# Float32r products of 128 rows as pairs of 64-row products on the two row halves of TensorE

## The chip, the cores and the metric

The kernel runs on one core of a Trainium2 chip (TensorE, VectorE, ScalarE, GpSimdE, SyncE and the DMA engines of that core). The metric is the device time of one launch in microseconds (us). The profile's names are used for the engines: PE is TensorE's matmuls, PEld its weight loads, DVE is VectorE, ACT is ScalarE, POOL is GpSimd, SP is SyncE, whose queue issues most DMAs.

## The reference

Windowed causal attention over 8 batches and 8 heads (576 positions, head dimension 64), and then a gated feed-forward network over all 4608 tokens. All data is float32.

```python
scores = np.where(mask, scale * q @ k.T + bias, -1e9)      # rel >= 0 and rel < 128
attn = softmax(scores) ; x = attn @ v                       # x: 4608 x 512
gate = 1.0 / (1.0 + np.exp(-(x @ w_gate)))                  # 512 x 1536
val = x @ w_val                                             # 512 x 1536
out = gate * val @ w_out                                    # 1536 x 512
```

## The kernel before

The program has four stages on PE: attention (scores, transposes, values), the first feed-forward blocks (line L913), the remaining feed-forward blocks (L1103), and last the product with `w_out` (L1290). Only the last stage changes.

The last stage multiplies a 3 x 3 grid of blocks by a scheme that needs fewer block products than the plain one: 15 products, named 0 to 14, over sums and differences of blocks of the hidden layer. It runs three times (`last(t)` for t = 0, 1, 2, called a third below), each for 1536 tokens. In a third the 15 products follow each other in the order of the text of `last`. They add into PSUM accumulators, the chains "A" to "F", with two banks each (j = 0 and 1, the two halves of 128 output columns). After a product, `then(j)` takes what is wanted out of its bank: a copy on ACT (`snap`, L1215; `fork`, L1220) or a multiply-add on DVE (`plus`, L1233).

A product has a contraction of 512, cut in four chunks of 128 rows. Float32 is kept by splitting each operand in a high and a low float32r part and multiplying three of the four pairs. So one product and one j is a group of 12 matmuls, each of 128 rows, 128 stationary columns and 512 moving columns into one PSUM bank; such a matmul with its weight load is called a record here. There are 15 x 3 x 2 = 90 groups. The moving operand is `duo`, a ring of four buffers (`RING`), two for each product (q = 0 and 1, two chunks each). The high part is a cast (`copy`, L326 on ACT or L327 on DVE) or a negated copy (L1256), the low part a subtraction on DVE (`minus`, L335, or L1257). Before some products `sums` (L1191) forms differences of blocks, on DVE, each on two halves. Products 13, 3 and 7 have one such pair of operations, products 4, 1 and 14 two. The stationary operand is `wo`, prepared earlier. `load` fetches blocks by DMA.

The order of all instructions is made by a planner, `Graph.order`: `g.add` gives each operation its engine, an assumed cost, what it reads and writes, and a priority (`want`). PE work in the order of the text has one priority (1.0e6); the planner takes what is ready first. Each engine then runs its instructions strictly in the planned order, with semaphores between engines.

At the very end (t = 2, product 14) the group j = 1 is done in two pieces of 256 columns (`last_six`, L1277). The key "seam" makes the first group of the last stage come behind matmuls of L1103 that read it.

Of the kernel before, what the change touches and what calls it, by code (L numbers as in the profile page):

```python
# [8 lines left out]
F32 = mybir.dt.float32  # L9
# [6 lines left out]
P = 128  # L16
B, H, S, D = 8, 8, 576, 64
# [7 lines left out]
NB = 512  # L25
# [10 lines left out]
NB9 = NT // NB  # L36
# [14 lines left out]
POOL = (0, 1, 6, 7)  # L51
# [16 lines left out]
EAGER, WARM = 30.0, 45.0  # L68
NEAR = 4.0
END = 2 * P  # L70
COLD, SLOW = 10.3, 0.85
FIRST_LAND = 0.9
LATE = 4.0
# [92 lines left out]
class Graph:  # L166
# [122 lines left out]
    def emit(self, o):  # L289
        o.made = o.emit()  # L290
        if o.after:
            self.tc.add_manual_dep(o.made.ins, o.after.made.ins.name, mybir.DependencyInfo(mybir.DependencyClass.Sync, mybir.DependencyReason.DATA), reason="port")
# [11 lines left out]
def attention_gated_ffn(ctx: ExitStack, tc: tile.TileContext, qd, kd, vd, wg, wv, wo, out):  # L304
    nc = tc.nc
# [61 lines left out]
    nc.gpsimd.iota(rel[:, 0], [[-1, P]], base=0, channel_multiplier=1, allow_small_or_imprecise_dtypes=True)  # L367
    ident = const.tile([P, P], F32, name="ident")
    make_identity(nc, ident)
    little = const.tile([P, TRI], F32, name="little")  # L370
    nc.gpsimd.memset(little, 1.0e-9)
    spare = {}
# [797 lines left out]
    def kept_at(slot):  # L1170
# [3 lines left out]
        n = 4 if tag[0] == "h" else 1  # L1174
        return T(moe, f"part_{tag}", [P, n, NB], F32, tag=tag)[:, i]

    def last(t):
        F = FIRST + 2
        rows, left = {}, {}

        def load(name, of=None):
            slots = [stage_free.pop(0) for _ in range(2)]
            rows[name] = slots
            for q, slot in enumerate(slots):
                move(lambda slot=slot: staged(slot), lambda q=q: hid[of or name, t, q],
                     [hid_key(of or name, t, 2 * q + m, i) for m in range(2) for i in range(4)], [("row", *slot)], F, 512, True)
# [7 lines left out]
        def drop(*names):  # L1194
            for name in names:
                stage_free.extend(rows.pop(name))
# [14 lines left out]
        def snap(name, chain, j):  # L1211
            keep_at((name, j))
            b = bks[chain, j]
            o = val((name, j))
            g.add("ACT", act_cost(NB, psum=True), lambda: nc.scalar.mul(o(), mm[b], 0.5), [("mm", b)], [key((name, j))], F)  # L1215
# [6 lines left out]
        def plus(o, chain, a, j, scale=0.5, op=ADD, fresh=False, cols=slice(NB)):  # L1222
            b, va = bks[chain, j], val((a, j))
            if fresh:
                keep_at((o, j))
                writes, reads = [key((o, j))], [key((a, j))]
                vo = val((o, j))
            else:
                writes, reads, vo = [key((a, j))], [], va
                held_at[o, j] = held_at.pop((a, j))  # L1230
            n = cols.stop - (cols.start or 0)
            b, at = (apart[0], slice(n)) if apart and cols.start else (b, cols)
            g.add("DVE", dve_cost(n, psum=True), lambda: nc.vector.scalar_tensor_tensor(  # L1233
                vo()[:, cols], mm[b][:, at], scale, va()[:, cols], op0=ALU.mult, op1=op), [("mm", b), *reads], ["tail"] if apart and cols.start else writes, F)
# [4 lines left out]
        def store(name, m, n, j, cols=slice(NB)):  # L1239
            r, c = (2 * m + j) * P, (3 * t + LABEL[3 * t:3 * t + 3].index(n)) * NB  # L1240
            v = val((name, j))
            x, y = cols.start or 0, cols.stop
            move(lambda: out[r:r + P, c + x:c + y], lambda: v()[:, cols], ["tail" if x else key((name, j))], [("out", r, c + x)], F, (y - x) / 2)
            if y == NB:
                free(name, j)

        def product(p, chain, name, then, minus_=False):
            ring = []
            for q in range(2):
                slot = rows[name][q]  # L1250
                r = RING[ducks[0] % len(RING)]
                ducks[0] += 1
                duo = lambda part_, r=r: T(moe, f"duo{r}", [P, 2, 2, NB], F32R, tag=f"ar{HOME[r]}")[:, part_]
                hi, lo, v = (lambda duo=duo: duo(0)), (lambda duo=duo: duo(1)), (lambda slot=slot: staged(slot))
                if minus_:
                    g.add("ACT", act_cost(2 * NB), lambda hi=hi, v=v: nc.scalar.mul(hi(), v(), -1.0), [("row", *slot)], [("ar", r, 0)], F)  # L1256
                    g.add("DVE", dve_cost(2 * NB, two=True), lambda hi=hi, lo=lo, v=v: nc.vector.scalar_tensor_tensor(  # L1257
                        lo(), v(), -1.0, as32(hi()), op0=ALU.mult, op1=SUB), [("row", *slot), ("ar", r, 0)], [("ar", r, 1)], F, port=True)
                else:
                    copy(hi, v, 2 * NB, [("row", *slot)], [("ar", r, 0)], F)  # L1260
                    minus(lo, v, lambda hi=hi: as32(hi()), 2 * NB, [("row", *slot), ("ar", r, 0)], [("ar", r, 1)], F, pool=False)
                ring.append((r, duo))
            for j in range(2):
                start = (chain, j) not in bks
                if start:
                    bks[chain, j] = bank()
                b = bks[chain, j]
                if t == NB9 // 3 - 1 and p == ORDER[-1] and j:
                    plus("a1", chain, "a1", j, cols=slice(END, NB))
                    apart.append(bank())  # L1270
                    for cols, b, at in ((slice(0, END), b, slice(0, END)), (slice(END, NB), apart[0], slice(0, NB - END))):
                        def last_six(cols=cols, b=b, j=j, at=at):
                            for q, (r, duo) in enumerate(ring):
                                for m in range(2):
                                    for e, (xp, wp) in enumerate(((0, 0), (0, 1), (1, 0))):
                                        z, i, part_ = unit(p, 2 * q + m, wp)
                                        nc.tensor.matmul(mm[b][:, at], wo2(z, part_)[:, i, j * P:(j + 1) * P], duo(xp)[:, m, cols],  # L1277
                                                         start=cols.start > 0 and q == m == e == 0, stop=q == 1 and m == 1 and e == 2, skip_group_check=True)
                        g.add("PE", 12 * ((cols.stop - cols.start) / 2400 + 0.0133), last_six,
                              [("ar", r, x) for r, _ in ring for x in range(2)] + sorted({("wo", *unit(p, k, w)[::2]) for k in range(KC) for w in range(2)}), [("mm", b)], 1.0e6)  # L1280
                        then(j, cols)
                    continue
                for q, (r, duo) in enumerate(ring):
                    units = {(m, w): unit(p, 2 * q + m, w) for m in range(2) for w in range(2)}

                    def six(q=q, duo=duo, b=b, j=j, units=units, start=start):
                        for m in range(2):
                            for e, (xp, wp) in enumerate(((0, 0), (0, 1), (1, 0))):
                                z, i, part_ = units[m, wp]
                                nc.tensor.matmul(mm[b], wo2(z, part_)[:, i, j * P:(j + 1) * P], duo(xp)[:, m],  # L1290
                                                 start=start and q == 0 and m == 0 and e == 0, stop=q == 1 and m == 1 and e == 2, skip_group_check=True)
                    g.add("PE", 6 * (NB / 2400 + 0.0133), six, [("ar", r, 0), ("ar", r, 1)] + sorted({("wo", z, part_) for z, _, part_ in units.values()}),
                          [("mm", b), *(["seam"] if t == 0 and p == ORDER[0] else [])], 1.0e6)
                then(j)
# [19 lines left out]
        sums("q2", "q2", "10", SUB)  # L1314
        product(4, "F", "q2", lambda j: plus("y11", "F", "a2", j))
        drop("q2")
        product(9, "E", "12", lambda j: (plus("y11", "E", "y11", j, -0.5), store("y11", 1, 1, j), snap("y12", "E", j)))
        drop("12")
        load("00")
        product(6, "B", "00", lambda j: (plus("y00", "B", "y00", j), store("y00", 0, 0, j)))  # L1320
        if t == 0:
            g.add("PY", 0.0, lambda: None, [("row", *rows["01"][1])], ["first rows"], F)
            for z in range(len(SLOTS), len(SLOTS) + len(LATER)):
                fetch_o(z, ["first rows"])
        load("q10")
        product(10, "C", "q10", lambda j: plus("y12", "C", "y12", j), True)
        load("22")
        sums("00", "22", "00", SUB)
        product(7, "B", "00", lambda j: plus("y02", "B", "y02", j))
        sums("q10", "01", "q10", SUB)  # L1330
        drop("01")
        sums("q10", "q10", "00", SUB)
        product(1, "C", "q10", lambda j: (plus("y02", "C", "y02", j), store("y02", 0, 2, j)))
        drop("q10")
        product(8, "B", "22", lambda j: (plus("y12", "B", "y12", j), store("y12", 1, 2, j)))
        drop("22")
        load("q5")
        sums("q5", "10", "q5", SUB)
        sums("q5", "q5", "00", SUB)
# [173 lines left out]
```

## Time and profile before

| | |
|---|---|
| median of 3 runs | 937.11 us (936.88 to 937.45) |
| profiled execution | 937.64 us, of which the span from first to last instruction is 935.9 us |
| PE | 926.5 us busy (99% of the span) |
| DVE | 783.9 us busy (84%) |
| ACT | 516.2 us busy (55%) |
| POOL | 207.5 us busy (22%) |

The sum of the prediction is made against the profiled execution's own 937.64 us, 0.53 us above the median. A busy share is an average over all stages: PE is without a gap in the last stage, and POOL's 22% lies almost all before it.

### The profile page before, as it was taken

How to read it: one execution, taken by the hardware profiler on the slowest of the kernel's cores; microseconds unless marked ns; L12 is line 12 of the kernel's file. 1: busy time of each engine (PE TensorE's matmuls, PEld its weight loads, DVE VectorE, ACT ScalarE, POOL GpSimd, SP SyncE). 2: the span in 40 equal slices, each digit the busy share in tenths (PEclk: the TensorE clock that was granted, in tenths of full speed). 3: DMA queues.
4: the chain of work that ended last, by engine and by line, in shares of the span. 5: the costliest groups of instructions: out<-in, count | busy, mean ns of one | idle time of the engine just before them, and what ended most of it. 6: DMA issues, size and time to landing. Idle time of an engine off the chain costs nothing.

```text
span 935.9 us, 18859 instructions
## 1 busy us (share of the span) xinstructions
PE 926.5 (99%) x6602; PEld 790.5 (84%) x6602; DVE 783.9 (84%) x1855; ACT 516.2 (55%) x1334; POOL 207.5 (22%) x394
## 2 busy tenths in 40 slices
PE   8999999999999999999999999999999999999998
PEld 7888888888878888888889999988888888888887
DVE  7999888898898998867888696774698998898896
ACT  8998888899874454324454363544454343333432
POOL 5644436554631000103021212212110000000000
PEclk9999999999999999999999999999999999999999
DMA  8787668966756445579798889879798571463531
GB/s 322 243 275 257 219 225 291 302 222 222 238 136 218 166 145 152 119 217 225 220 224 282 241 218 336 201 222 303 199 286 277 155 277 57 158 223 148 157 113 68
DMA packets 91631, 200.27 MB, mean 214 GB/s; under 512 B 10000, under 2 KB 28688, under 8 KB 91152
## 3 DMA queue, kind: packets, MB, share of 16 engines
q1 hardware_dynamic: 79728, 179.86, 56.4%
q0 software_dynamic: 11520, 18.88, 13.5%
q8 instruction: 52, 0.85, 0.4%
q10 hardware_dynamic: 288, 0.33, 0.1%
q14 instruction: 43, 0.35, 0.1%
HBM read 118.03 MB, written 81.00 MB: 213 GB/s over the span
## 4 chain that ended last, share of the span: by engine, by line
PE 92%; DVE 3%; ACT 1%; POOL 1%; issue 1%; DMA 1%; POOLq 0%; DVEq 0%
PE mm L1103 23%; PE later L1103 22%; PE later L1290 15%; PE mm L1290 10%; PE mm L913 9%; PE area L671 4%; PE mm L734 3%; PE mm L785 3%; PE mm L823 1%; POOL pt L796 1%; ACT pb L582 1%; DVE area L688 1%; DVE pb L578 1%; PE mm L783 1%; DVE pb L775 0%
## 5 line engine op out<-in xcount | busy, mean ns | idle before, releaser
L1103 PE MATMUL later<-xc,w2s 128*128 128x512 f32 (+1 forms) x1008 | 225.4, 371 | 0.0
L1103 PE MATMUL mm<-xc,w2s 128*128 128x512 f32 (+1 forms) x1008 | 225.0, 371 | 0.0
L1103 PEld LDWEIGHTS mm<-xc,w2s 128*128 128x128 f32 x1008 | 184.7, 188 | 26.4 <-DVE later_hs L1120 0.2
L1103 PEld LDWEIGHTS later<-xc,w2s 128*128 128x128 f32 x1008 | 184.6, 188 | 26.5
L913 PE MATMUL mm<-first,first 128*128 128x512 f32 x480 | 127.1, 404 | 0.0
L1290 PE MATMUL later<-duo,wo 128*128 128x512 f32 x432 | 100.7, 389 | 0.0
L861 POOL DMA_DIRECT2D hidq<-later_hs x47 | 41.2, 905 | 260.9 <-DVE later_hs L1120 141.0
L913 PEld LDWEIGHTS mm<-first,first 128*128 128x128 f32 x480 | 85.1, 189 | 16.0 <-ACT spread L326 0.6
L1290 PEld LDWEIGHTS later<-duo,wo 128*128 128x128 f32 x432 | 81.1, 188 | 16.8
L582 ACT ACTIVATE pb<-pb,st 128x128 f32<-128x128 f32 x216 | 84.7, 396 | 3.6 <-DVE st L578 3.0
L1290 PE MATMUL mm<-duo,wo 128*128 128x512 f32 x324 | 75.7, 389 | 0.0
L1290 PEld LDWEIGHTS mm<-duo,wo 128*128 128x128 f32 x324 | 60.8, 188 | 12.6
L1115 ACT ACTIVATE sg<-later 128x512 f32<-128x512 f32 (+3 forms) x55 | 27.4, 512 | 57.1 <-PE later L1103 40.9
L796 POOL TENSOR_SCALAR_AFFINE_SELECT pt<-early_h 128x384 f32<-128x384 f32 x96 | 49.3, 536 | 40.4 <-ACT early_h L326 14.4
L796 POOL TENSOR_SCALAR_AFFINE_SELECT pt<-spread 128x384 f32<-128x384 f32 x96 | 49.4, 540 | 38.4 <-ACT spread L326 15.3
L1115 ACT ACTIVATE sg<-mm 128x512 f32<-128x512 f32 (+3 forms) x53 | 27.5, 526 | 49.0 <-PE mm L1103 36.2
L734 PEld LDWEIGHTS mm<-pt,vr 64*64 64x64 f32 x1056 | 41.1, 133 | 10.5 <-POOL st L765 3.2
L1110 DVE TENSOR_TENSOR later<-later,low 128x512 f32<-128x512 f32 (+1 forms) x48 | 31.3, 652 | 21.9 <-PE later L1103 21.5
L326 ACT COPY low<-mm 128x512 f32<-128x512 f32 (+1 forms) x45 | 24.6, 550 | 45.2 <-PE mm L1103 29.3
L1110 DVE TENSOR_TENSOR mm<-mm,low 128x512 f32<-128x512 f32 (+1 forms) x48 | 31.2, 651 | 19.4 <-PE mm L1103 16.8
L734 PE MATMUL mm<-pt,vr 64*64 64x192 f32 (+2 forms) x1056 | 45.2, 284 | 0.8 <-POOL pt L796 0.8
L578 DVE CUSTOM_DVE_ANT_0 pb<-area,early_h 128x128 f32<-128x128 f32 x198 | 45.2, 286 | 0.7
(258 smaller groups left out, 1646.7 us busy)
## 6 DMA issues: line engine op xcount, KB each, us to landing
hid<-later_hs SPq DMA_DIRECT2D x38, 256.0 KB, 3.6
vr<-in_v_dram SPq DMA_DIRECT2D x32, 288.0 KB, 5.0
hidq<-later_hs POOLq DMA_DIRECT2D x36, 256.0 KB, 6.0
wraw<-in_moe_w_gate_dram SPq DMA_DIRECT2D x14, 512.0 KB, 5.1
wraw<-in_moe_w_val_dram SPq DMA_DIRECT2D x14, 512.0 KB, 4.8
wraw<-in_moe_w_out_dram SPq DMA_DIRECT2D x12, 512.0 KB, 6.1
rows_xr<-hidq SPq DMA_DIRECT2D x11, 512.0 KB, 5.0
w2s<-stash SPq DMA_DIRECT2D x6, 896.0 KB, 9.5
```

Source lines behind the costliest of these rows:

```text
L578: g.add("DVE", 0.21, lambda: nc.vector.tensor_tensor_reduce(pb()[:, e], from_(), relm[u.p][:, w], op0=ALU.add, op1=ALU.min, scale=-0.125, ...
L582: g.add("ACT", 0.39, lambda: nc.scalar.activation(pb()[:, e], pb()[:, e], AF.Exp, bias=st()[:, e:e + 1], scale=-1.0, accum_out=st()[:, 3 + ...
L671: nc.tensor.matmul(squares()[h * D:(h + 1) * D, a:a + n], qraw(u)[rows, i - r * MID, h * D:(h + 1) * D], keys, start=True, stop=True)
L734: nc.tensor.matmul(mm[both[h].at][e * D:(e + 1) * D, a - e * S - cuts[h]:b - e * S - cuts[h]], vraw(u)[r * D:r * D + D, c], seen, start=fi ...
L785: nc.tensor.transpose(mm[z.at][:, e * P:(e + 1) * P], pb()[:, e], ident)
L796: return nc.gpsimd.affine_select(pt(u)[:, f0:f0 + 2 * n - 1:2, :], both(), [[0, n], step], cmp, 0.0, base=0, channel_multiplier=mult)
L861: g.add("POOL", 1.2, lambda to=to, of=of: nc.gpsimd.dma_start(to(), of(), accum_op=ALU.add), keys, parts_, F, size=2 * kb / 300.0, port=False)
L913: nc.tensor.matmul(mm[s.at][:, 0:wd], w.tile(kind, wi, i)[:, c * P:(c + 1) * P], xpart(x, c)[:, 0:wd], start=(k == 0 and c == 0), stop=(k ...
L1103: nc.tensor.matmul(mm[b][:, 0:N2], w.tile2(i, wp)[:, wk, c * P:(c + 1) * P], combo(k, xp, N2)[:, c], start=(start and c == 0 and j == 0), ...
L1110: g.add("DVE", dve_cost(N2, psum=True), lambda: nc.vector.tensor_tensor(o(), bk(b)(), a(), op=ALU.add), [("mm", b), *reads] if okeys else ...
L1115: g.add("ACT", act_cost(y - x, psum=True), lambda x=x, y=y, s=s: nc.scalar.activation(sg[h]()[:, x:y], bk(b)()[:, x:y], AF.Tanh, scale=0.5 ...
L1290: nc.tensor.matmul(mm[b], wo2(z, part_)[:, i, j * P:(j + 1) * P], duo(xp)[:, m], start=start and q == 0 and m == 0 and e == 0, stop=q == 1 ...
```

## The change

In the last stage every record but those of the very last product for j = 0 and 1 at t = 2 becomes two matmuls of 64 rows: one on rows 0 to 63 (r = 0), one on rows 64 to 127 (r = 1). 88 groups (1056 records) become 2112 half matmuls. Both halves of a record add into the same bank. The half on rows 64 to 127 is issued 16 records behind (8 steps of two records, `BEHIND`), so that the two halves that stand next to each other in the program mostly write different banks. Where a group's second half begins, it waits for a semaphore of POOL: a memset of one column of a small tile `passed`, which itself waits for the end of the group's first half. `then(j)` is planned after the group's second half. Before the very last product, `run_out` issues the 16 outstanding second halves alone. The order of the 12 records in a group is changed (four records with the high part of `duo` stand first), and the order of the products in a third is changed in its second half.

```diff
+BEHIND = 8
+    passed = const.tile([P, 4], F32, name="passed")
...
+    def step(now, extra=()):
+        line.append(now)
+        then_ = line[-1 - BEHIND] if len(line) > BEHIND else []
+        def matmuls():
+            for k in range(2):
+                for r, recs in enumerate((now, then_)):
+                    if not recs:
+                        continue
+                    group, emit, _, _, n = recs[k]
+                    made = emit(slice(r * D, r * D + D), r == 0 and n == 0, r == 1 and n == 11)
+                    if r == 0:
+                        group.end = made
+                    elif n == 0:
+                        tc.add_manual_dep(made.ins, group.passed.ins.name, SYNC, reason="halves")
+        recs = now + then_
+        g.add("PE", 2 * NB / 2400, matmuls, sorted({k for x in recs for k in x[2]}), sorted({x[3] for x in recs}) + list(extra), 1.0e6)
+        for k, then in [x for x in due if x[0] == len(line) - 1]:
+            then()
+        due[:] = [x for x in due if x[0] > len(line) - 1]
+    def run_out():
+        for _ in range(BEHIND):
+            step([])
...
+                if not ends:
+                    recs, group = [], Group()
+                    for q, (r, duo) in enumerate(ring):
+                        for m, xp, wp in ((0, 0, 0), (0, 0, 1), (1, 0, 0), (1, 0, 1), (0, 1, 0), (1, 1, 0)):
+                                z, i, part_ = unit(p, 2 * q + m, wp)
+                                def emit(rows, first, final, z=z, i=i, part_=part_, xp=xp, m=m, duo=duo, b=b, start=start, j=j):
+                                    return nc.tensor.matmul(mm[b], wo2(z, part_)[rows, i, j * P:(j + 1) * P], duo(xp)[rows, m], start=start and first,
+                                                            stop=final, skip_group_check=True)
+                                recs.append((group, emit, [("ar", r, xp), ("wo", z, part_)], ("mm", b), len(recs)))
+                    for k in range(0, 12, 2):
+                        step(recs[k:k + 2], ["seam"] if t == 0 and p == ORDER[0] else [])
...
+                    g.add("POOL", 0.12, passing, [("mm", b)], [("passed", x)], F, port=False)
+                    due.append((len(line) - 1 + BEHIND, lambda j=j: then(j)))
                     continue
...
+        load("00")
+        product(6, "B", "00", lambda j: (plus("y00", "B", "y00", j), store("y00", 0, 0, j)))
         product(9, "E", "12", lambda j: (plus("y11", "E", "y11", j, -0.5), store("y11", 1, 1, j), snap("y12", "E", j)))
...
         product(7, "B", "00", lambda j: plus("y02", "B", "y02", j))
+        load("q10")
+        product(10, "C", "q10", lambda j: plus("y12", "C", "y12", j), True)
+        product(8, "B", "22", lambda j: (plus("y12", "B", "y12", j), store("y12", 1, 2, j)))
```

The products of a third stood in the order 11, 2, 13, 0, 12, 3, 5, 4, 9, 6, 10, 7, 1, 8, 14; now 11, 2, 13, 0, 12, 3, 5, 4, 6, 9, 7, 10, 8, 1, 14.

**PE, third and fourth group of the last stage, before.** These are the twelve records of one group and the start of the next (`later` and `mm` are PSUM banks, the number tells them apart).

```order
L1290 MATMUL later_4118<-duo_7446,wo_7308 128x512 [waits Activation_49]
L1290 MATMUL later_4118<-duo_7446,wo_7223 128x512
L1290 MATMUL later_4118<-duo_7446,wo_7308 128x512 [waits DVE_49]
L1290 MATMUL later_4118<-duo_7446,wo_7363 128x512
L1290 MATMUL later_4118<-duo_7446,wo_7286 128x512
L1290 MATMUL later_4118<-duo_7446,wo_7363 128x512
L1290 MATMUL mm_71<-duo_7437,wo_7180 128x512
```

The same place after the change:

```order
L1328 MATMUL later_4119<-duo_7447,wo_7364 128x512
L1328 MATMUL later_4118<-duo_7426,wo_7152 128x512
L1328 MATMUL later_4120<-duo_7438,wo_7181 128x512
L1328 MATMUL later_4118<-duo_7426,wo_7244 128x512
L1328 MATMUL later_4120<-duo_7438,wo_7092 128x512
...
L1328 MATMUL later_4120<-duo_7438,wo_7181 128x512
L1328 MATMUL later_4119<-duo_7438,wo_7181 128x512 [waits Pool_49]
L1328 MATMUL later_4120<-duo_7438,wo_7244 128x512
L1328 MATMUL later_4119<-duo_7438,wo_7092 128x512
```

First halves of one group now alternate with second halves of an earlier one, each pair in two banks. The second half of a group (bank 4119) starts behind a wait for POOL, while the first half of the next group (bank 4120) is under way; everything behind that wait in PE's queue, both halves, stands too.

**POOL, end of its program, before** (`hidq` is DRAM, filled by DMAs that POOL issues and that add to what is there):

```order
L861 DMA hidq_170<-shared 128x512 [waits DMASW5_49,DMASW0_49,DVE_49]
L861 DMA hidq_171<-later_hs_7172 128x512 [waits DMAHW6_49,DMASW6_49,DVE_49]
L861 DMA hidq_171<-later_hs_7172 128x512 [waits DMASW7_49,DMASW6_49,DVE_49]
L1508 UNCONDITIONAL_BRANCH
```

After:

```order
L863 DMA hidq_172<-later_hs_7173 128x512 [waits DMAHW6_49,DMASW6_49,DVE_49]
L1336 MEMSET passed 128x1 [waits PE_49] x3
L863 DMA hidq_172<-later_hs_7173 128x512 [waits DMASW7_49,DMASW6_49,DVE_49]
L1336 MEMSET passed 128x1 [waits PE_49]
L1336 MEMSET passed 128x1 [waits PE_49,Pool_49] x84
L1568 UNCONDITIONAL_BRANCH
```

The 88 memsets are new, and 85 of them stand behind the last DMA that POOL issues.

**DVE, end of the first third, before** (`rows_` are blocks of the hidden layer, `part_` are results that are being added up; L1233 empties a bank, L1191 is a sum, L335 makes the low part for the ring):

```order
L1233 SCALAR_TENSOR_TENSOR part_h_7720<-later_4119,part_h_7720 128x512 [waits PE_49]
L1191 TENSOR_TENSOR rows_xr<-rows_xr,rows_ar_7483 128x1024 [waits DVE_49]
L335 TENSOR_TENSOR duo_7399<-rows_wraw_6615,duo_7399 128x1024 [waits Activation_49]
L1233 SCALAR_TENSOR_TENSOR rows_tt<-later_4116,rows_tt 128x512 [waits PE_49]
L335 TENSOR_TENSOR duo_7425<-rows_xr,duo_7425 128x1024 [waits Activation_49]
L1191 TENSOR_TENSOR rows_tt<-rows_xr,rows_tt 128x1024 [waits DMAHW1_49]
```

After, in the same part of the third:

```order
L1268 SCALAR_TENSOR_TENSOR part_h_7918<-mm_73,part_h_7918 128x512 [waits PE_49]
L1226 TENSOR_TENSOR rows_wraw_6616<-rows_xr,rows_wraw_6616 128x1024 [waits DMAHW4_49]
L336 TENSOR_TENSOR duo_7400<-rows_ar_7471,duo_7400 128x1024 [waits PE_49,Activation_49]
L1268 SCALAR_TENSOR_TENSOR part_h_7918<-mm_74,part_h_7918 128x512 [waits DVE_49,PE_49]
L1226 TENSOR_TENSOR rows_wraw_6616<-rows_wraw_6616,rows_ar_7471 128x1024 [waits DVE_49]
L1268 SCALAR_TENSOR_TENSOR rows_tt<-later_4119,rows_tt 128x512 [waits PE_49]
L336 TENSOR_TENSOR duo_7426<-rows_wraw_6616,duo_7426 128x1024 [waits Activation_49]
```

The work is of the same kinds and in the same mixture. What moved is what it waits for: the low part into the ring (`duo_7400`) now waits for PE as well, since the ring buffer is read for 16 records longer, and each emptying of a bank waits for the second half of its group, with sums and low parts behind it.

## Rows read from the trace of the kernel before

**Rows 1.** The cores: span and mean granted TensorE clock.
```profile
core 0: 935.9 us, clock 1.000
```
**Rows 2.** The chain that ended last: start us, us, what.
```profile
501.60 3.12 PE later L1103 x18
...
736.03 32.64 PE later L1290 x144
```
**Rows 3.** The same chain, asked for 680 to 740 us: where the last stage begins.
```profile
679.82 5.89 PE mm L1103 x26
685.71 1.36 PE later L1290 x6
687.07 1.36 PE mm L1103 x6
688.43 6.80 PE later L1290 x30
```
**Rows 4.** Groups of instructions from 684 us on, shapes apart: busy us, mean ns.
```profile
L1290 PE MATMUL later<-duo,wo 128*128 128x512 f32 x432 | 100.7, 389 | 0.0
L1290 PEld LDWEIGHTS later<-duo,wo 128*128 128x128 f32 x432 | 81.1, 188 | 16.8
...
L326 ACT CAST duo<-rows_xr 128x1024 fp32r<-128x1024 f32 x18 | 19.0, 1053 | 25.7 <-PE mm L1290 16.3 <-PE later L1290 7.0 <-DVE rows_xr L1191 2.0
```
**Rows 5.** Stretches of the last stage: busy us of each engine, granted clock.
```profile
740.00:760.00 20.00, 20.00 (x90) 16.57 (x89) 20.00 (x22) 8.36 (x8) 0.00 (x0) 1.00 0.69 214
...
820.00:840.00 20.00, 20.00 (x90) 16.57 (x89) 20.00 (x22) 6.94 (x7) 0.00 (x0) 1.00 0.68 218
...
900.00:920.00 20.00, 20.00 (x90) 16.57 (x89) 20.00 (x23) 7.14 (x7) 0.00 (x0) 1.00 0.22 67
...
688.00:929.00 241.00, 241.00 (x1065) 199.53 (x1065) 215.10 (x224) 89.96 (x102) 2.07 (x2) 1.00 0.53 175
```
**Rows 6.** DVE in order of time: start us, us, what.
```profile
744.99 1.22 DVE L1191 TENSOR_TENSOR rows_xr<-rows_hs,rows_xr 128x1024 f32<-128x1024 f32 x1
746.12 1.22 DVE L1191 TENSOR_TENSOR rows_wraw<-rows_wraw,rows_wraw 128x1024 f32<-128x1024 f32 x1
747.25 0.69 DVE L1233 SCALAR_TENSOR_TENSOR part_h<-later,part_h 128x512 f32<-128x512 f32 x1
747.85 1.22 DVE L1191 TENSOR_TENSOR rows_xr<-rows_xr,rows_ar 128x1024 f32<-128x1024 f32 x1
748.99 1.22 DVE L335 TENSOR_TENSOR duo<-rows_wraw,duo 128x1024 fp32r<-128x1024 f32 x1
```
**Rows 7.** PE in order of time: scores of one attention unit, and six transposes.
```profile
61.35 1.54 PE L671 MATMUL area<-early_h,early_xr 64*64 64x64 f32 x44
...
82.09 0.82 PE L785 MATMUL mm<-ident,pb 128*128 128x128 f32 x6
```
**Rows 8.** PE's groups over those scores, shapes apart, and the transposes of the whole trace.
```profile
L671 PE MATMUL area<-early_h,early_xr 64*64 64x192 f32 x20 | 1.5, 325 | 0.0
L671 PE MATMUL area<-early_h,early_xr 64*64 64x128 f32 x12 | 1.4, 274 | 0.0
L671 PE MATMUL area<-early_h,early_xr 64*64 64x64 f32 x12 | 1.2, 226 | 0.0
...
L785 PE MATMUL mm<-ident,pb 128*128 128x128 f32 x192 | 30.6, 279 | 0.3 <-DVE st L767 0.2
```
**Rows 9.** Weight loads of those scores, in order of time and as a group.
```profile
61.35 1.40 PEld L671 LDWEIGHTS area<-early_h,early_xr 64*64 64x64 f32 x44 [0.17 <-DVE wbits L494]
...
L671 PEld LDWEIGHTS area<-early_h,early_xr 64*64 64x64 f32 x44 | 1.4, 133 | 0.2 <-DVE wbits L494 0.2
```
**Rows 10.** POOL: its shortest memsets as a group, and its last two DMAs in order of time.
```profile
L1497 POOL MEMSET const-float32-0.0<- 128x1 f32 x1 | 0.1, 98 | 0.3 <-issue 0.3
...
688.99 0.85 POOL L861 DMA_DIRECT2D hidq<-later_hs  x1 [5.26 <-DVE later_hs L1120]
698.11 1.22 POOL L861 DMA_DIRECT2D hidq<-later_hs  x1 [8.27 <-DVE duo L327]
```

More of the change, by code (lines that the diff above doesn't have):

```diff
@@ L1175, in kept_at @@
         return T(moe, f"part_{tag}", [P, n, NB], F32, tag=tag)[:, i]
+    class Group:
+        end = passed = None
+    SYNC = mybir.DependencyInfo(mybir.DependencyClass.Sync, mybir.DependencyReason.DATA)
+    line, due, turns2 = [], [], [0]
+    def step(now, extra=()):
[20 more added lines that the diff above has]
+            step([])
     def last(t):
@@ L1262, in product @@
                 ring.append((r, duo))
+            ends = t == NB9 // 3 - 1 and p == ORDER[-1]
+            if ends:
+                run_out()
             for j in range(2):
@@ L1267, in product @@
                 b = bks[chain, j]
-                if t == NB9 // 3 - 1 and p == ORDER[-1] and j:
+                if ends and j:
                     plus("a1", chain, "a1", j, cols=slice(END, NB))
@@ L1281, in product, with passing @@
                         then(j, cols)
+                    continue
+                if not ends:
[9 more added lines that the diff above has]
+                        step(recs[k:k + 2], ["seam"] if t == 0 and p == ORDER[0] else [])
+                    x = turns2[0] % 4
+                    turns2[0] += 1
+                    def passing(x=x, group=group):
+                        group.passed = nc.gpsimd.memset(passed[:, x:x + 1], 0.0)
+                        tc.add_manual_dep(group.passed.ins, group.end.ins.name, SYNC, reason="halves")
+                        return group.passed
+                    g.add("POOL", 0.12, passing, [("mm", b)], [("passed", x)], F, port=False)
+                    due.append((len(line) - 1 + BEHIND, lambda j=j: then(j)))
                     continue
@@ L1316, in last @@
         drop("q2")
+        load("00")
+        product(6, "B", "00", lambda j: (plus("y00", "B", "y00", j), store("y00", 0, 0, j)))
         product(9, "E", "12", lambda j: (plus("y11", "E", "y11", j, -0.5), store("y11", 1, 1, j), snap("y12", "E", j)))
         drop("12")
-        load("00")
-        product(6, "B", "00", lambda j: (plus("y00", "B", "y00", j), store("y00", 0, 0, j)))
         if t == 0:
@@ L1324, in last @@
                 fetch_o(z, ["first rows"])
-        load("q10")
-        product(10, "C", "q10", lambda j: plus("y12", "C", "y12", j), True)
         load("22")
@@ L1329, in last @@
         product(7, "B", "00", lambda j: plus("y02", "B", "y02", j))
+        load("q10")
+        product(10, "C", "q10", lambda j: plus("y12", "C", "y12", j), True)
+        product(8, "B", "22", lambda j: (plus("y12", "B", "y12", j), store("y12", 1, 2, j)))
+        drop("22")
         sums("q10", "01", "q10", SUB)
@@ L1334, in last @@
         drop("q10")
-        product(8, "B", "22", lambda j: (plus("y12", "B", "y12", j), store("y12", 1, 2, j)))
-        drop("22")
         load("q5")
```

## The prediction, made before the run

> **What bounds the kernel now.** I read the core's span and clock first: 935.9 us, at a mean granted clock of 1.000 [rows 1]. By the page's shares PE is busy for 99% of that span. Then the chain that ended last, and its start of the last stage: from 685.71 us on the chain is PE alone, piece after piece of L1290 with no other engine between [rows 2, 3]. The table of stretches shows the same, 241.00 of 241 us busy on PE, at a granted clock of 1.00, TensorE's upper level of 2.4 GHz [rows 5]. So the stage's length is the number of records times the distance of one from the next. 144 records take 32.64 us, 226.7 ns each; the 18 records of 384 columns in L1103 take 3.12 us, 173.3 ns each [rows 2]. 512 columns at 2.4 GHz are 213.3 ns and 384 are 160.0: in both a record costs 13.3 ns beyond its columns. That fixed part is all that the change can win.
>
> Next to PE stands DVE. Over the stage it is busy for 215.1 of 241 us, which looks like slack, but the stretches 740 to 760, 820 to 840 and 900 to 920, each near the end of a third, have 20.00 of 20 [rows 5]. There DVE runs back to back: two-input operations of 1024 elements follow each other by 1.13 us, a bank of 512 is emptied in 0.60 [rows 6]. An average hides this; it decides what a later release of a bank costs.
>
> **Part 1: the distance of records.** 1056 records become pairs of half matmuls with 2112 weight loads. If the two halves of a pair run side by side, columns alone cost 213.3 ns a pair; if the pair keeps the whole fixed part, 226.7. These are the bounds for halves that overlap. Nothing in the stage shows matmuls on row halves, but the scores do, on 64x64 tiles: 44 records, 20 of 192 columns, 12 of 128, 12 of 64, 6144 columns, done in 1.54 us [rows 7, 8]. Spread over four tiles that is 1536 columns each. The transposes of 128 columns take 0.82 us for six where one alone lasts 0.28 [rows 7, 8], so (0.82 − 0.28)/5 = 108 ns for 128 columns: f32 columns cost two cycles, 106.7 ns, plus 1.3 ns. The 1536 columns are then 1.28 us, and of the 1.54 about 0.17 is the tail of the last (226 ns, less its own 53 ns of columns). What is left, 0.09 us over 11 records a tile, is at most 8 ns a record, start included. So tiles do run side by side (four times 1.28 us in 1.54), and two kinds of PE work with a weight load before every matmul have a fixed part of 1.3 and of at most 8 ns. Against this, both are plain f32; that the 13.3 ns come from 128 rows, and not from float32r itself, no row shows.
>
> I take 1.5 ns, 214.8 ns a pair, nearer to the transposes, since their figure is the cleaner: 1056 x (226.7 − 214.8) = **12.5 us gained**. At 8 ns (221.3) it would be 5.7, at the bounds 14.1 and 0.
>
> Weight loads double. A load of 64 columns lasts 133 ns in the scores, and 44 of them lie within 1.40 us, so they overlap about fourfold [rows 9]; one of 128x128 lasts 188 ns [rows 4]. I cost the doubling at nothing, since the cover is the other half's matmul; without the cover, see rival C. The Trainium skill (TensorE: Matmul & The Clock Gate, Part 3: Packing small matmuls) says that row tiles run concurrently and start some 4 ns apart, and that weight loads overlap matmuls in flight only where the row group differs. The same page (Back-to-back issue gap) gives 2.5 ns beyond the columns for an isolated matmul, where L1290 shows 13.3. With 2.5 ns the pair is an estimated 215.8 ns and the forecast below would end near 935.5.
>
> **Part 2: filling and emptying.** The second half runs 16 records behind, so 16 records at the start and 16 at the end of the stage have one half only: 32 half steps where 16 full ones would do, **16 x 0.2148 = 3.4 us lost**. This is arithmetic, if a lone half costs the columns of a pair.
>
> **Part 3: DVE's work at the end of each third.** Here two things meet. With shorter records PE gets through the last five products in 120 x 0.2148 = 25.8 us, before 27.2. DVE's work there is 10 low parts and 10 sums at 1.13 and 10 bank emptyings at 0.60, 28.6 us [rows 6]: before, 1.4 us more than PE, which the ring's lead absorbed; now 1.4 us more on top. And every bank is ready, and every ring buffer free, 16 records (3.4 us) later. The slack for that is thin. The q = 0 buffer was last read at record 18 of 24 and is needed again at 48 (its high part): 30 records, 6.8 us. Now it is read until 34, and 14 records are left, 3.0 us. In that time come a cast of 1.05 us [rows 4] and, by record 52, a subtraction of 1.22 [rows 6]: 1.6 us to spare, if DVE is free. It isn't: in DVE's queue the bank emptyings, now later, stand ahead of sums and low parts, and all behind one that waits, waits too. A wait of PE at the end of each third is new therefore. Bounds: 0 per third, if the ring's lead absorbs it as before; 1.3 + 3.4 = 4.7, if shortage and lag both show in full. I take 2.0, a little under the middle, as the lag is a delay and not work, and comes back once DVE is ahead again: **3 x 2.0 = 6.0 us lost**. The changed order of products makes up a part of this; it changes no count.
>
> **Part 4: the gate on POOL.** 88 memsets of one column, 98 ns for the nearest one [rows 10], on an engine with 2.07 us of work in the whole stage [rows 5]. A first half begins at step 0 of its group, its last record begins 11 steps later and lasts 389 ns [rows 4]: it ends at 11 x 0.2148 + 0.39 = 2.75 us. The second half starts at 16 x 0.2148 = 3.44. That leaves 0.69, and less a weight load ahead of the matmul about 0.5 us, for PE to POOL, the 98 ns, and POOL to PE. I cost it at nothing, with that 0.5 as cover. One place is tighter: POOL's last DMA starts at 698.11, after 8.27 us of idleness [rows 10], and now stands ahead of the fourth memset. That group's first half ends about 48 records behind the stage's start at 687 to 688 us [rows 3], at about 697.9. Behind the DMA of 1.22 us the gate may open up to 1.5 us late. I take **0.4 us lost** (0 to 1.5).
>
> The seam: six records of L1290 stood between two groups of L1103 [rows 3] and now come behind both. No count changes: nothing. The other order of the 12 records costs nothing on PE either; what it changes is counted in part 3.
>
> **Sum.** 12.5 − 3.4 − 6.0 − 0.4 = 2.7 us gained. 937.64 − 2.7 = 934.9 for an execution like the profiled one; less 0.53 for the median, **934.4 us**, 0.3% less than before. The lowest difference a measurement of this kernel can tell from no change is about 0.2%, 1.87 us.
>
> **The rivals.**
>
> *A, the forecast:* halves overlap, a pair at 213.3 to 217 ns. With part 3 as taken this gives 932.8 to 936.8. Chance 0.60.
>
> *B, slower:* the 13.3 ns are float32r's own price, paid in each half, and since the halves go in step the pair stays at 226.7 ns. For it speaks that both shapes of float32r pay just this [rows 2] and no plain f32 does. Then part 1 is nothing, filling costs 16 x 0.2267 = 3.6, the shortage at the thirds' ends is no larger than before so that I put 1.0 for each there, and POOL 0.4: 3.6 + 3.0 + 0.4 = 7.0, 944.1 us. It decides from a pair of 217.3 ns on: there 1056 x (226.7 − p) just pays 16 x p + 6.4 us. Chance 0.24.
>
> *C:* weight loads of the two halves go one behind another. 64 columns more lengthen a load from 133 to 188 ns [rows 4, 9], so 128 columns cost 110 ns, two of them 220 per pair: 7.1 − 3.5 − 4.5 (part 3 between A's and B's) − 0.4 = −1.3, 938.4 us. The fourfold overlap of the scores' loads speaks against it. Chance 0.05. The Trainium skill (TensorE: Matmul & The Clock Gate, LDWEIGHTS) says that a load's time is set by its columns, so that one of half the rows takes as long; rows 9 show no load of 64 rows with 128 columns.
>
> *D, the change doesn't do what it says:* halves that write 512 columns each don't run side by side, some 430 ns a pair, over 200 us more, about 1150. The scores speak against it. Chance 0.03.
>
> *E:* the gate is late in every group; each 0.2 us beyond its cover is 88 x 0.2 = 17.6 us, 952 us. No row shows PE waiting for POOL. Chance 0.05.
>
> *F:* DVE keeps up at the thirds' ends: 12.5 − 3.4 − 0.4 = 8.7, 928.4 us. Chance 0.03.
>
> **How the numbers follow.** Faster by over 0.2% (below 935.2): 0.47 of A's 0.60 and F's 0.03, 0.50. Within 0.2%: 0.12 of A, 0.03 of C, 0.01 each of B and E, 0.17. Slower: 0.01 of A, 0.23 of B, 0.02 of C, 0.03 of D, 0.04 of E, 0.33. The range runs from 931.0, which holds pairs at the lower bound with waits of 1.4 us a third, to 944.6, which takes in B; D, E, F and the ends of A lie outside, under 2 in 10. A's own range is 932.8 to 936.8.
>
> **What the profile after would show.** The distance of pairs in a stretch without waits, in the chain's rows of L1328: 215 ns for A, 227 for B, 220 for C, 430 for D. PE idle for about 2 us at the end of each third, ended by DVE (low part or emptied bank): part 3; no such idleness is F. PE idle at second halves, ended by POOL: E; once, near 698 us: part 4. Lone halves at the stage's start and end at the same distance as pairs: part 2. What would make me wrong most easily is the fixed part, of which every 1 ns is worth 1.06 us, then the waits of part 3, three times whatever one of them is.

## The result, and the profile after

| | before | after |
|---|---|---|
| median, us | 937.28 (936.88 to 938.27, 4 runs) | 946.35 (945.96 to 947.32, 4 runs) |
| ratio | | 1.0097 (95% interval 1.0079 to 1.0114) |
| span of the profiled execution, us | 935.9 | 945.6 |

The changed kernel is slower by 9.1 us, 1.0%. The forecast was 934.4 us, 0.3% faster; the range ended at 944.6.

The cores, and the chain that ended last from 680 us on (start us, us, what), answer to [rows 1 to 3]:

```profile
core 0: 945.6 us, clock 1.000
```

```profile
697.22 1.24 DVE duo L336
698.46 1.87 issue
700.33 0.86 POOL hidq L863
701.35 4.84 PE later L1328 x39
...
767.16 1.05 ACT duo L327
768.24 1.24 DVE duo L336
769.52 0.49 PE mm L1328
...
771.18 18.13 PE mm L1328 x160
```

Two things are to be seen. First the price of a pair: 160 half matmuls follow each other in 18.13 us, 113.3 ns each, **226.6 ns a pair**. That is within 0.1 ns of what a record of 128 rows took in [rows 2]. Second, the chain, which before was PE alone, now leaves PE: at 698 us for a DMA on POOL, at 767 us for a cast on ACT and a low part on DVE. PE stands still at the first place like this (idle before, releaser in brackets):

```profile
701.35 3.94 PE L1328 MATMUL later<-duo,wo 64*128 64x512 f32 x32 [1.86 <-POOL passed L1336]
```

The stretches (PE busy, PEld, DVE, ACT, POOL, PEclk, DMA share, GB/s) answer to [rows 5]:

```profile
740.00:760.00 20.00, 20.00 (x179) 17.29 (x177) 19.12 (x22) 7.73 (x9) 0.69 (x7) 1.00 0.70 227
820.00:840.00 20.00, 20.00 (x180) 16.54 (x178) 18.76 (x21) 7.15 (x8) 0.69 (x7) 1.00 0.61 179
900.00:920.00 20.00, 20.00 (x178) 16.51 (x178) 18.39 (x21) 8.35 (x9) 0.69 (x7) 1.00 0.34 106
```

In 20 us there were 90 records, and there are 180 halves now: no more work in the same time. DVE, at 20.00 of 20 before, is at 18.4 to 19.1: it stands idle for 0.9 to 1.6 us in each of these stretches, although (as the experiments show) it is short of time there.

Two groups of that stage, shapes apart (busy us, mean ns | idle before, releaser; an L1328 matmul has 64 rows), answer to [rows 4]:

```profile
L1328 PE MATMUL later<-duo,wo 64*128 64x512 f32 x901 | 137.9, 386 | 1.9 <-POOL passed L1336 1.9
L1328 PEld LDWEIGHTS later<-duo,wo 64*128 64x128 f32 x899 | 111.8, 184 | 18.8 <-POOL passed L1336 2.3
```

A half lasts 386 ns where a whole record lasted 389, and its weight load 184 where that of 128 rows lasted 188. Half the rows make neither notably shorter.

**Where the 9.1 us went.** From the first half matmul of L1328 (687.18 us) to the first matmul of L1350 (935.83) are 248.65 us. 1056 pairs and the 16 more steps of filling and emptying, at 226.67 ns, are 242.99; the other 5.66 us are waits of PE: 2.1 at 701 us, 1.4 at 761 to 770, 1.3 at 851 to 853, the rest in small pieces. (These are counted from start to start, beyond the 226.67 ns; the idle time that a row shows in brackets is shorter, as the last matmul's end overlaps the next start.) 16 x 0.2267 = 3.6 us of filling and 5.7 of waits are 9.3, of a difference of 9.7 between the two spans of the profiled executions. Nothing was won on the other side.

### The profile page after: what moved, and what is told of

Its sections match the earlier page's. It is cut to its first block, busy times and chain, and to the rows that moved or that the text cites. A ratio compares the mean times of both kernels' runs of the same rounds, so it can differ in the third digit from the quotient of the medians.

```text
span 945.6 us, 21145 instructions
## 1 busy us (share of the span) xinstructions
PE 933.0 (99%) x7658; PEld 794.7 (84%) x7658; DVE 782.1 (83%) x1849; ACT 522.0 (55%) x1340; POOL 215.7 (23%) x482
## 5 line engine op out<-in xcount | busy, mean ns | idle before, releaser
L1328 PE MATMUL later<-duo,wo 64*128 64x512 f32 x912 | 140.5, 387 | 1.9 <-POOL passed L1336 1.9
L1328 PEld LDWEIGHTS later<-duo,wo 64*128 64x128 f32 x912 | 114.1, 184 | 19.6 <-POOL passed L1336 2.3
L1328 PE MATMUL mm<-duo,wo 64*128 64x512 f32 x600 | 97.7, 386 | 0.0
L1328 PEld LDWEIGHTS mm<-duo,wo 64*128 64x128 f32 x600 | 78.6, 184 | 11.8
L1336 POOL MEMSET passed<- 128x1 f32 x88 | 9.0, 102 | 229.3 <-PE later L1328 128.2
L736 PEld LDWEIGHTS mm<-pt,vr 64*64 64x64 f32 x1056 | 41.1, 133 | 10.5 <-POOL st L767 3.2
```

Source lines behind the costliest of these rows:

```text
L736: nc.tensor.matmul(mm[both[h].at][e * D:(e + 1) * D, a - e * S - cuts[h]:b - e * S - cuts[h]], vraw(u)[r * D:r * D + D, c], seen, start=fi ...
L1328: return nc.tensor.matmul(mm[b], wo2(z, part_)[rows, i, j * P:(j + 1) * P], duo(xp)[rows, m], start=start and first, stop=final, skip_grou ...
L1336: group.passed = nc.gpsimd.memset(passed[:, x:x + 1], 0.0)
```

## The experiments

**Where do the 13.3 ns come from?** The forecast rested on their being hidden by two halves side by side; rival B held that they are float32r's own price. The first kernel changes the kind of the records in the kernel before, a kind for each third (shortened):

```diff
+if t == 0:   w, x = (y.bitcast(mybir.dt.bfloat16)[:, 1::2] for y in (w, x))
+elif t == 1: w, x = as32(w), as32(x)
+elif 0 < 6 * q + 3 * m + e < 11: w, o = w[:, 0:D], mm[b][0:D]
-nc.tensor.matmul(mm[b], wo2(z, part_)[...], duo(xp)[:, m], ...)
+nc.tensor.matmul(o, w, x, ...)
```

> The kernel before, its last stage in three kinds: in the first third both operands of every record are bfloat16 views (the upper halves of the same numbers), in the second third plain float32 views, in the third third records 1 to 10 of each group use 64 of the 128 stationary columns. Outputs lose precision or parts; only the distance of records is asked for. Theory (the 13.3 ns beyond the columns are float32r's own price for each matmul): bfloat16 about 213.3 + 2.5 = 216 ns, float32 at two cycles a column 426.7 + 2.5 = 429 ns, 64 stationary columns still 226.7 ns. Rival 1 (price of every matmul with new weights over 128 rows, whatever the type): 226.7, 440, 226.7. Rival 2 (price of bringing in 128 stationary columns): 226.7, 440, 220. Total by the theory: 360 x (429 - 226.7) = +73 us and at most -4 us, about 1006 us; by the rivals 1012 to 1014 us.

Measured: 1165.9 us (one run). The chain, one row of each third:

```profile
735.94 32.64 PE later L1297 x144
768.58 30.90 PE mm L1297 x72
...
1088.60 8.26 PE later L1297 x36
```

bfloat16 read with a step takes 226.7 ns, just as float32r: my theory fell, and with it rival B's reason. Plain float32 takes 30.90/72 = 429.2 ns, that is two cycles a column (426.7) and 2.5 ns, so rival 1 fell too. (The total was far off since a plain float32 record stands in the trace as two such matmuls: 360 x (858.4 - 226.7) = 227 us more.) With 64 stationary columns in ten of twelve records the distance is 8.26/36 = 229.4, no shorter, so the columns of the weight load are not it either.

What bfloat16 with a step shares with float32r is that the columns of the moving operand lie 4 bytes apart. The next kernel takes that away (shortened):

```diff
+if t == 0:   w, x = w.bitcast(half)[:, 1::2], x.bitcast(half)[:, 1::2]
+elif t == 1: w, x = w.bitcast(half)[:, 1::2], x.bitcast(half)[:, 0:NB]
+else:        w, x = w.bitcast(half)[:, 0:P], x.bitcast(half)[:, 1::2]
```

> The kernel before with every record of the last stage in bfloat16, views of the high parts only (the low parts are left out): in the first third both operands are read with a step of two elements (4 bytes), in the second third the moving operand is packed, in the third third the stationary one (packed views hold other numbers). The run before showed 226.7 ns for the stepped views, as for float32r. Theory (the fixed 13.3 ns belong to any matmul of one pass that brings its own weights): 226.7 in all three. Rival 1 (reading 4 bytes per column costs it): about 216 ns in the second third only. Rival 2 (loading the weights costs it): about 216 ns in the third third only. Total: 937 us by the theory, 933 us by either rival.

Measured: 934.5 us (one run; before 937.8 beside it). The chain in each third:

```profile
736.04 32.64 PE later L1298 x144
...
779.04 7.77 PE mm L1298 x36
...
858.09 8.13 PE later L1298 x36
```

226.7, **215.8** and 225.8 ns. With the moving operand packed, 10.9 of the 13.3 ns go, and 2.5 stay; packing the weights changes next to nothing. Rival 1 holds: at one column a cycle, a matmul whose moving columns lie 4 bytes apart pays about 11 ns more. Two things stay open. The packed view also spans half the bytes, and no run parts the distance of the columns from that. And float32r numbers are 4 bytes wide themselves and can't be packed closer: that this is the reason for float32r too is inferred from the equal price (226.7 ns). Why the price is the same for 256 columns (24 matmuls of L1315 in 2.88 us, 120.0 ns each), 384 and 512, the runs don't tell. The Trainium skill (TensorE: Matmul & The Clock Gate, Back-to-back issue gap) gives 2.5 ns beyond the columns for an isolated matmul; the packed third and plain float32 agree with it, float32r (13.3) doesn't.

The same in the changed kernel, with float32r, packed and stepped bfloat16 in the three thirds (shortened):

```diff
+if t == 1:   w, x = ...[rows].bitcast(half)[:, 1::2], duo(0)[rows, m].bitcast(half)[:, 0:NB]
+elif t == 2: w, x = w.bitcast(half)[:, 1::2], x.bitcast(half)[:, 1::2]
```

> The changed kernel (pairs of 64 rows) in three kinds: float32r in the first third as it is; in the second third bfloat16 with the moving operand packed (high parts only, the packed view holds other numbers, the low parts are left out); in the third third bfloat16 views read with a step of 4 bytes, as in the run of the kernel before. Theory (the 13.3 ns belong to a matmul that reads its moving columns 4 bytes apart at one column a cycle, and each half reads its own): pairs at 226.7, about 216 and 226.7 ns where PE doesn't wait. Rival (two halves side by side are held to 226.7 ns by something of their own, such as two weight loads for each pair): 226.7 in all three.

Measured: 942.3 us (one run), and in the chain:

```profile
713.43 18.63 PE later L1335 x164
...
795.75 17.27 PE mm L1335 x160
...
849.88 18.00 PE later L1335 x160
```

Two halves make a pair: 227.2, **215.9** and 225.0 ns. A pair costs what one record of 128 rows of the same kind costs, within 0.5 ns in the first two kinds; stepped bfloat16 is 1.7 ns cheaper in pairs (225.0 against 226.7), which stays open. Halves run side by side in full, but neither hides the other's fixed part. That they start together is not the reason. In most of the changed kernel's stage the two start 3 ns apart, but in the last third of this run 0.10 us apart, when about half of the columns of the one are still to come:

```profile
870.55 0.38 PE L1335 MATMUL mm<-duo,wo 64*128 64x512 bf16 x1
870.65 0.38 PE L1335 MATMUL later<-duo,wo 64*128 64x512 bf16 x1
870.78 0.38 PE L1335 MATMUL mm<-duo,wo 64*128 64x512 bf16 x1
```

From one half to the next on the same rows it is about 0.225 us all the same. Each half of the rows keeps its own distance, wherever the other stands.

**Is the gate on POOL late?** `BEHIND = 8` became 7, and then 6.

> The changed kernel with the second half 14 records behind instead of 16 (BEHIND = 7). Theory (the gate on POOL has almost no margin: in the trace after, the memset ends 65 ns before the second half's first matmul): the second half could start 0.45 us earlier and the gate can't, so PE waits some 0.4 us in each of 88 groups, 34 to 40 us, less 0.45 us of filling: 980 to 986 us. Rival (the prediction's margin of 0.5 us at 16 records, 0.05 us at 14): no waits, 945.5 to 946 us.

Measured: 946.7 us (one run). The theory was a wrong reading: the 65 ns were from the memset to the next matmul of any group. The weight load that really waits for POOL began 0.31 us after the memset's end with 16 records, and 0.05 us after it with 14, in each of the four groups I read (in the whole trace 0.05 to 0.07 us in 87 of 88 groups with 14, in the median 0.31 with 16); no matmul was late for it. So 14 records are just enough, and 16, two records or 0.45 us more, have about the cover of 0.5 us that the prediction gave them.

> The changed kernel with the second half 12 records behind (BEHIND = 6). At 14 records the weight load that waits for the memset began 0.05 us after the memset's end in each group, and no matmul was late; at 16 it began 0.31 us after it. Theory (the gate opens at a fixed time after the group's first half, so at 12 it is 0.45 us late for the load and some 0.2 to 0.4 us for the matmul): 88 x 0.2 to 0.4 = 18 to 35 us more, 964 to 981 us. Rival (PE has room that the profile doesn't show): 945 to 947 us.

Measured: 974.3 us (one run). PEld's waits (us in total, times, longest us):

```profile
PEld later L1328 <- POOL passed L1336: 24.7, 49, 1.9
PEld mm L1328 <- POOL passed L1336: 18.2, 38, 0.5
```

One of these loads in order of time (idle before, releaser in brackets):

```profile
714.20 0.18 PEld L1328 LDWEIGHTS mm<-duo,wo 64*128 64x128 f32 x1 [0.48 <-POOL passed L1336]
```

87 of 88 loads wait, 0.5 us each, and the time rises by 27.6 us over 14 records (single runs), about 0.31 us for each group. So rival E's mechanism is real, and begins between 14 and 12 records; at 16 it is not there.

**What makes the waits at the thirds' ends?** Three kernels. In the first, one of the differences ahead of product 14 is left out in the first third:

```diff
-sums("q5", "q5", "00", SUB)
+if t > 0:
+    sums("q5", "q5", "00", SUB)
```

> The changed kernel without the second of the two differences ahead of product 14 in the first third (two operations of 1.13 us on DVE less, that part of the output differs). Theory (DVE runs out of time at a third's end): the wait of some 1.2 us at 768 us goes, the one of the second third at 851 us stays, 945.1 us. Rival (the ring's buffer comes free too late, 16 records later than before): both waits stay, 946.3 us.

Measured: 947.9 us (943.8 to 948.9, 4 runs), too far apart to tell 1 us. The trace decides. PE's waits in the changed kernel, and in this one, at the ends of the first and the second third (idle before, releaser in brackets):

```profile
768.26 0.50 PE L1328 MATMUL mm<-duo,wo_ar 64*128 64x512 f32 x1 [0.66 <-ACT duo L327]
851.29 0.49 PE L1328 MATMUL later<-duo,wo_ar 64*128 64x512 f32 x1 [0.69 <-ACT duo L327]
```

```profile
852.83 0.50 PE L1328 MATMUL later<-duo,wo_ar 64*128 64x512 f32 x1 [0.72 <-ACT duo L327]
```

The first is gone, the second stays. In this run PE also stood longer at 701 us (2.65 us), which could have given DVE a lead; the two kernels further down, without any wait there, rule that out. With whole records in products 11 and 2, PE waits at both ends (at 766 and at 849 us); with the difference left out as well, in the first two thirds, at neither. All waits of PE from 686 us on, of the one and of the other (us in total, times, longest us):

```profile
PE later L1328 <- ACT duo L327: 0.7, 1, 0.7
PE mm L1328 <- ACT duo L327: 0.7, 1, 0.7
PE later L1328 <- DVE duo L1292: 0.6, 1, 0.6
```

```profile
PE later L1328 <- DVE duo L1292: 0.6, 1, 0.6
```

DVE's time is what is missing. In the changed kernel DVE works without a gap from 757.2 us up to the difference that the cast reads; its last two operations there and ACT's cast:

```profile
765.23 0.69 DVE L1268 SCALAR_TENSOR_TENSOR part_h<-mm,part_h 128x512 f32<-128x512 f32 x1
765.83 1.22 DVE L1226 TENSOR_TENSOR rows_wraw<-rows_wraw,rows_ar 128x1024 f32<-128x1024 f32 x1
```

```profile
767.16 1.05 ACT L327 CAST duo<-rows_wraw 128x1024 fp32r<-128x1024 f32 x1 [3.43 <-PE later L1328]
```

The releaser named for ACT is PE, but the cast starts 0.11 us after DVE's difference into `rows_wraw` ends (767.05): the difference was last.

The second kernel is the one before with the new order of products alone:

> The kernel before with the changed order of products alone, records of 128 rows. Theory 1 (the order brings the double differences of products 1 and 14 next to each other on DVE, and this makes the waits at the thirds' ends): PE waits up to 1.2 us at the end of the first and second third, up to 939.5 us. Theory 2 (the lag of 16 records makes them): no waits, 937.1 us.

Measured: 938.00 us against 937.89, ratio 1.0002 (0.9993 to 1.0012). PE has no wait in the stage, though DVE is as full as before:

```profile
740.00:760.00 20.00, 20.00 (x90) 16.57 (x89) 19.96 (x23) 7.94 (x9) 0.00 (x0) 1.00 0.72 221
820.00:840.00 20.00, 20.00 (x90) 16.55 (x89) 19.97 (x22) 8.47 (x9) 0.00 (x0) 1.00 0.66 212
```

The order alone costs nothing. (The changed kernel with the old order wasn't tried: products 8 and 14 would follow each other in chain "B", and halves of two groups would meet in one bank.) The third kernel has `BEHIND = 12`:

> The changed kernel with the second half 24 records behind (BEHIND = 12). Filling: 8 x 0.2267 = 1.8 us more. Theory 1 (the waits at the thirds' ends are a lag of DVE's queue): they grow by up to 1.8 us each at the first and second end, 949.9 to 951.8 us in all. Theory 2 (they are a shortage of DVE time that the lag doesn't change): 948.2 us.

Measured: 949.85 us, ratio to before 1.0135 (1.0120 to 1.0151). By the ratios that is 3.5 us more than with 16 records, 1.8 of filling and 1.7 of waits. Its trace shows the waits grow (us in total, times, longest us):

```profile
PE later L1328 <- ACT duo L327: 1.7, 2, 0.8
PE mm L1328 <- ACT duo L327: 0.8, 1, 0.8
PE mm L1328 <- DVE duo L1292: 0.8, 1, 0.8
```

These are four waits of 0.8 us, at 762, 836, 847 and 930 us, the last in the last third, where with 16 records there was none. With 16 records there are two of 0.7, with 14 two of 0.5. Together: DVE has no time to spare at a third's end, and lives off its lead; each record of lag takes from the lead. Neither of the two alone makes PE wait.

**The wait at 701 us.** Products 11 and 2 of the first third are done as before, so that no memset stands near POOL's last DMA:

```diff
-if not ends:
+if not ends and not (t == 0 and p in (11, 2)):
```

> The changed kernel, but products 11 and 2 of the first third (48 records) are done as before, with records of 128 rows; so no memset stands near POOL's last DMA. Theory (one wait of 2.0 us at 699 us, for that DMA ahead of the fourth memset): it goes, 944.3 us. Rival (PE would wait there or later for something else anyway): 946.3 us.

Measured: 945.62 us, ratio 1.0083 (1.0068 to 1.0098), by the ratios 1.3 us better than the change, though the two intervals overlap. The 2.0 us are gone, but at 722.5 us there is a new wait of some 0.8, for a low part on DVE that stood behind a bank's emptying:

```profile
720.66 0.69 DVE L1268 SCALAR_TENSOR_TENSOR rows_tt<-later,rows_tt 128x512 f32<-128x512 f32 x1 [1.61 <-PE later L1328]
721.27 1.22 DVE L1292 SCALAR_TENSOR_TENSOR duo<-rows_wraw,duo 128x1024 fp32r<-128x1024 f32 x1
```

The edit made this wait itself: in the changed kernel the two stand the other way round in DVE's queue.

```profile
721.76 1.22 DVE L1292 SCALAR_TENSOR_TENSOR duo<-rows_wraw,duo 128x1024 fp32r<-128x1024 f32 x1
723.46 0.69 DVE L1268 SCALAR_TENSOR_TENSOR rows_tt<-later,rows_tt 128x512 f32<-128x512 f32 x1 [0.48 <-PE later L1328]
```

With 14 records, and in the run with packed bfloat16, whose first third is that of the changed kernel, PE waited neither at 701 us nor here.

**Both edits together** (this edit, and the difference ahead of product 14 left out in the first two thirds):

> The changed kernel with products 11 and 2 of the first third as before (128 rows) and without the second of the two differences ahead of product 14 in the first and second third (part of the output differs): both known sources of waits are gone. Theory (what is left of the loss is the filling, 16 x 0.2267 = 3.6 us, and one wait of some 0.7 us at 722 us for a low part on DVE): 937.5 + 4.3 = 941.8 us. Rival (the pairs win something after all, hidden by the waits so far): below 939 us.

Measured: 942.93 us, ratio 1.0055 (1.0038 to 1.0072), 5.1 us over before: filling 3.6, the wait at that low part 0.8 in its trace, and small pieces. The waits at 701 us and at the two thirds' ends are gone, and still the pairs win nothing.

## Why the prediction was wrong, point by point

- **Part 1 is the step that failed.** It took 1.5 ns beyond the columns and 12.5 us of gain. The pair stayed at 226.6 ns, and the gain was 0, the lower of its own two bounds. I sized the fixed part by the transposes and the scores [rows 7, 8], which are plain float32 at two cycles a column, and not by the nearest rows, float32r at 384 and 512 columns [rows 2]. The runs put 11 of the 13.3 ns on moving columns 4 bytes apart at one column a cycle, and a half reads them so as well. Of the 12.4 us between the 934.9 forecast for the profiled execution and its 947.32, this step is 12.5; part 4 adds 1.7, part 2 0.2 and small pieces about 1.2, and part 3, which was taken too large, hides 3.2 of it. That halves run side by side, and that the doubled weight loads cost nothing (rival C), was right.
- **Rival B** had the right distance and the wrong reason (bfloat16 with a step pays the same), and its 944.1 us was 2.2 short. Its 3.0 us for the thirds' ends were near the 2.8 measured; the wait on POOL and the small pieces are what it lacked.
- **Part 2**: 3.4 us predicted, 3.6 by the distance measured. Lone halves keep the distance of pairs: in the run-out seven follow each other like this, (1.75 − 0.39)/6 = 0.227 us each.

```profile
934.16 1.75 PE L1328 MATMUL later<-duo,wo_h 64*128 64x512 f32 x7
```

- **Part 3**: 2.0 us predicted for each third; measured 1.4, 1.3 and next to nothing. The mechanism was right (full DVE, lag, an in-order queue), and the size went with part 1: a PE that isn't faster doesn't outrun DVE by the 1.4 us counted there. In the packed run, whose pairs took 215.9 ns in the second third, PE lost 2.1 us at that third's end, about what I took for pairs of 214.8 ns (that kernel reads no low parts):

```profile
847.54 0.37 PE L1335 MATMUL later<-duo,wo_ar 64*128 64x512 bf16 x1 [1.95 <-ACT duo L327]
```

  That the last third waits next to nothing, perhaps because it has no next third to load and prepare for, was not tested.
- **Part 4**: the cover was right; the one wait near 698 us came at 701 and took 2.1 us, not 0.4 (bound 1.5). POOL's last DMA began 2.2 us later than in [rows 10], and with it the memset. I had taken that start as fixed:

```profile
695.70 0.10 POOL L1336 MEMSET passed<- 128x1 f32 x1 [2.62 <-PE later L1328]
700.33 0.86 POOL L863 DMA_DIRECT2D hidq<-later_hs  x1 [4.53 <-issue]
700.87 0.43 POOL L1336 MEMSET passed<- 128x1 f32 x1
```

In other executions of kernels with the same POOL program that DMA began at 698.1 (packed run), 699.2 (14 records) and 701.7 us (one difference less). It follows the landing of POOL's DMA before it: in the traces of all twelve kernels of this case it starts 0.6 or 0.9 us after that landing. Before, that DMA was issued at 688.99 and landed 8.5 us later; after, at 688.27, and landed 11.2 us later:

```profile
DMA to landing us min/median/max: 8.5/8.5/8.5
```

```profile
DMA to landing us min/median/max: 11.2/11.2/11.2
```

With 7.9 us (14 records) and 8.1 us (packed run) PE had no wait here, with 10.5 us (24 records) it stood for 0.48 us, with 12.0 us (one difference less) for 2.65. (With 12 records, where no gate has cover, it stood for 1.53 us at a landing of 8.1.) So the wait comes and goes with that transfer, and the lower times of the changed kernel may be without it. Why the landing takes 7 to 12 us is open.

## What to carry to other kernels

Before a fixed price for each instruction is taken as something that a second stream can hide, find the row that is nearest in type and layout to the work itself: here two shapes of float32r showed the same 13.3 ns, and rows of another type lured me away. Two half-height matmuls side by side cost what one whole matmul of their kind costs (within 2 ns, in the three kinds tried), so splitting a full one wins nothing here; what filling rows that would else stand empty is worth, these runs don't ask. A lag between the halves isn't free even where it hides nothing: its filling is paid at once, and every release behind it comes later, which shows where the engine that feeds the ring has no time to spare. And an edit that is to take one wait away can reorder the queue of another engine, so compare the order before a new wait is put down to the old one.

## What the runs showed of the hardware that was not expected

In the run with one difference less, PE stood idle for 2.65 us for POOL's gate, and the granted clock fell after it (stretches as above):

```profile
702.00:704.00 2.00, 1.31 (x10) 1.09 (x12) 0.00 (x0) 0.00 (x0) 0.63 (x2) 0.88 0.56 53
704.00:707.00 3.00, 3.00 (x18) 2.35 (x16) 2.69 (x3) 0.33 (x1) 0.10 (x1) 0.51 0.44 70
707.00:710.00 3.00, 3.00 (x30) 2.50 (x28) 2.70 (x3) 1.21 (x2) 0.10 (x1) 1.00 0.70 244
```

At 0.51, the lower of the two levels (1.2 GHz), seven pairs were about 427 ns apart instead of 227: another 1.4 us on top of the wait. After the 1.86 us of idleness in the changed kernel, and 1.95 in the packed run, the clock stayed at 1.00. The four times of that run lie 5 us apart, and the profiled execution was the slowest of them. Without the 3.0 us from start to start at this wait and the 1.8 at the lower clock and around it, its 948.86 would be an estimated 944.1, near the fastest of the four (943.76); that this is the reason is likely, but not shown.
